# A gated mixer on one core: the first row pair by Strassen too, with scaling, softmax factors and value copies on other engines

## The chip, the cores and the metric

One core of a Trainium2 chip runs the whole program. The metric is the device time of one execution in microseconds (us); the times shown are medians of several runs. A further execution was profiled.

## The reference

Two branches share one input x of 2048 tokens by 512, and a gate mixes them, all inputs in bf16:

```python
x = A_x
g = sigmoid((x * gate_w).sum(-1, keepdims=True))
# branch A: linear attention, 32 heads of 16
q, k, v = heads(x @ wqkv)
phi_q = concat(softmax(q @ w_phi), softmax(-q @ w_phi))     # per head, 32 features
phi_k = concat(softmax(k @ w_phi), softmax(-k @ w_phi))
kv, z = phi_k^T v, sum_s phi_k
a = (phi_q kv / (phi_q z + 1e-6)) @ wo
# branch B: gated MLP with a spatial product over the tokens
z = gelu(x @ w_in)                     # 2 x 688 columns
z1, z2 = z[:, :688], layernorm(z[:, 688:])
b = (z1 * (w_sp @ z2 + b_sp)) @ w_out  # w_sp: 2048 x 2048, entries of some 0.0005
out = g * a + (1 - g) * b
```

## The kernel before, in words

Tokens are handled in 16 tiles of 128. TensorE's and ScalarE's instructions run in the order in which they are written (a manual schedule); the scheduler orders those of VectorE, GpSimd and the SyncE queue (SP) by the order of writing and by when their inputs are ready. So the place of a statement in the loops below sets what waits for what.

**Gelu stage.** For 16 tiles z2 is computed (8 matmuls, gelu by ScalarE, statistics and normalisation by VectorE into `z2all`, fp16), then for 16 tiles z1 (`z1_tile`, L278). Both write to `zp`, two PSUM banks in three buffers. During z1 `fold` (L318) multiplies w_phi into the query and key weights, on PE and with three copies by ScalarE, and `z_sum` (L397) makes eight block sums T1 to T4 of z2all on VectorE.

**Key stage, 16 steps.** Each step `tt` does `k_tile(tt + 1)` and `v_tile(tt)` on TensorE, then `kv_acc(tt - 2)`, then its share of the spatial product, and in some steps (`Q_AT`) a `q_tile`. A key tile is two exponentials by ScalarE (`ek`, both signs), one sum per head by VectorE (`zs`, L446), a reciprocal (`rk`), and two GpSimd operations that give the second half of `ek` the ratio of the two sums (`even_out`). What is then left, the factor 1/z, VectorE multiplies into the value tile `vr` (L487) as it leaves PSUM, and GpSimd writes it to vr's last columns (L485).

**Spatial product.** w_sp is loaded transposed by DMA, by pairs: pair p holds row tiles p and p + 8 in one of four ring buffers (`w_load`, tile `wsp`). The pair's four blocks A11, A12 (row tile p) and A21, A22 are multiplied by the four blocks of z2all with Strassen's scheme in Winograd's form: seven `product`s of 8 matmuls each (L563) instead of eight. They need S1 = A21 + A22, S2 = A22 - S3, S3 = A11 - A21, S4 = A12 - S2 (`w_sum`), made on VectorE in fp16. To keep fp16 in range, a pair has a level: ScalarE sums the magnitudes (`w_size`, tile `mute`, L341), a matmul with ones sums over partitions (`w_level`), and VectorE forms `wdown` and its inverse `wup`. ScalarE scales the lower half by wup (`w_scale`, L374); the upper half stays raw in bf16 and is scaled inside the two sums that use it (`w_mul_sub`, L361). Product 1, made of raw numbers, is scaled when ScalarE copies it to a second bank (`seed`). Pair 0 doesn't do this: `plain` (L527) multiplies its rows in bf16, 16 matmuls for each half row, and one VectorE instruction finishes it. The finished rows are multiplied into z1all, for Strassen's pairs by GpSimd (`gated`, L577).

`steps` lists the products by step; `work_at` lists when sizes, scalings and sums are made ready: S3 and S1 of a pair one step before its first, S2 in it, S4 one later. The products use three PSUM banks (`mm0` to `mm2`), keys, values and queries one each (`mm3` to `mm5`).

**Output stage.** The rest of the products, the attention tiles (`attn_tile`), and for each token tile the two last products and the store (`ba_tile`) alternate by the list `FILL`.

Of the kernel before, what the change touches and what calls it, by code (L numbers as in the profile page):

```python
# [14 lines left out]
P = 128  # L15
S = 2048
D = 512
# [18 lines left out]
PLAIN = (0,)  # L36
MIXED = (1, 2, 3, 4, 5, 6, 7)
# [4 lines left out]
def kernel(  # L42
# [53 lines left out]
    wsum = pers.tile([P, NP, 2], FP32, name="wsum")  # L96
    wsum16 = pers.tile([P, NP], BF16, name="wsum16")
# [57 lines left out]
    nc.sync.dma_start(out=brow[0:NT, :], in_=B_b_sp.rearrange("(t p) -> t p", p=P))  # L155
    heads = A_w_phi.rearrange("(kc u) e f -> u e kc f", u=8)
    for qk in (1, 0):
        nc.sync.dma_start_transpose(
            out=wqkT[:, qk * NDT:(qk + 1) * NDT, :], in_=A_wqkv[:, qk * D:(qk + 1) * D])
        for u in range(8 if qk == 1 else 0):  # L160
            us = slice(u * DH, (u + 1) * DH)
            nc.sync.dma_start(out=wphi[us, :, us], in_=heads[u])
    nc.sync.dma_start(out=wv_sb[:, :, :], in_=A_wqkv[:, 2 * D:3 * D].rearrange("(dt p) n -> p dt n", p=P))
# [9 lines left out]
    for p in range(3):  # L173
        w_load(p)
# [163 lines left out]

    def w_size(p, h):
        mute = ring.tile([P, NT * P], BF16, name="mute", bufs=1)  # L340
        nc.scalar.activation(  # L341
            out=mute[:, :],
            in_=wraw[p][:, h * NT:(h + 1) * NT, :].rearrange("p s c -> p (s c)"),
            func=AF.Abs, accum_out=wsum[:, p, h:h + 1])
        if h == 1:
            nc.scalar.activation(
                out=wsum16[:, p:p + 1], in_=wsum[:, p, 1:2], func=AF.Identity, bias=wsum[:, p, 0:1])

    def w_level(p, ps):
        nc.tensor.matmul(ps[:, 0:1], lhsT=ones_sq[:, :], rhs=wsum16[:, p:p + 1], start=True, stop=True)  # L350
        with tc.high_priority():
            nc.vector.tensor_scalar(
                out=wdown[:, p:p + 1], in0=ps[:, 0:1], scalar1=LEVEL, scalar2=1e-30,
                op0=ALU.mult, op1=ALU.max)
            nc.vector.reciprocal(out=wup[:, p:p + 1], in_=wdown[:, p:p + 1])  # L355

    HALVED = (5, 6)

    def w_mul_sub(out, raw, p, minus):
        for c in (slice(0, HS // 2), slice(HS // 2, HS)) if p in HALVED else (slice(0, HS),):  # L360
            nc.vector.scalar_tensor_tensor(  # L361
                out=out[:, c, :], in0=raw[:, c, :], scalar=wup[:, p:p + 1], in1=minus[:, c, :],
                op0=ALU.mult, op1=ALU.subtract)

    def w_part(p, name):
        if name in ("S2", "S3"):
            return wmix[p][:, 0 if name == "S3" else 1]
        b = {"A11": 0, "A12": 1, "S4": 1, "S1": 2, "A21": 2, "A22": 3}[name]
        w = wraw[p] if name in ("A11", "A12") else wraw[p].bitcast(FP16)
        return w[:, b * HS:(b + 1) * HS, :]  # L370

    def w_scale(p):
        tail = wraw[p][:, NT:2 * NT, :].rearrange("p s c -> p (s c)")
        nc.scalar.activation(out=tail.bitcast(FP16), in_=tail, func=AF.Copy, scale=wup[:, p:p + 1])  # L374

    def w_sum(p, k):
        if k == 3:
            wmix[p] = ring.tile([P, 2, HS, P], FP16, name="wmix", bufs=2)
        a21, a22, s2, s3 = (w_part(p, name) for name in ("A21", "A22", "S2", "S3"))
        if k == 1:  # L380
            nc.vector.tensor_tensor(out=a21, in0=a21, in1=a22, op=ALU.add)
        elif k == 2:
            nc.vector.tensor_tensor(out=s2, in0=a22, in1=s3, op=ALU.subtract)
        elif k == 3:
            w_mul_sub(s3, w_part(p, "A11"), p, a21)
        else:
            w_mul_sub(w_part(p, "S4"), w_part(p, "A12"), p, s2)
# [15 lines left out]
    with tc.manual_schedule(engines={mybir.EngineType.PE, mybir.EngineType.Activation}):  # L403
        z2_first_two()
        for tt in range(2, NT):
            z2_tile(tt)
            if tt % 4 == 3:
                z2_norm(list(range(tt - 3, tt + 1)))
        b_T()
        turn["zp"] += 1  # L410
        for tt in range(NT):
            z1_tile(tt)
            if tt % 2 == 1:
                z_sum(tt // 2 // 4, tt // 2 % 4)
            if tt in (6, 11):
                later = fold(1 if tt == 6 else 0)
            if tt in (7, 8, 12, 13):
                later.pop(0)()

# [32 lines left out]
    def k_tile(tt, bank):  # L452
        ek, z = expo(kvp, "ek", 5, tt, wk_p, bank_tile(bank))
        rk = kvp.tile([P, H, 2], FP32, name="rk", bufs=3)
        nc.vector.reciprocal(out=rk[:], in_=z[:])  # L455
        even_out(ek, z, rk[:, :, 1])
        return ek, rk

    def even_out(e, z, rz):
        ratio = work.tile([P, H], FP32, name="ratio")  # L460
        nc.gpsimd.tensor_tensor(out=ratio[:], in0=z[:, :, 0], in1=rz, op=ALU.mult)  # L461
        nc.gpsimd.tensor_tensor(  # L462
            out=e[:, :, 1, :], in0=e[:, :, 1, :],
            in1=ratio[:, :, None].to_broadcast([P, H, DH]), op=ALU.mult)

# [3 lines left out]
    def q_tile(n, ps):  # L469
        eq, z = expo(work, "eq", 3, token(n), wq_p, ps)  # L470
        rq = work.tile([P, H], FP32, name="rq")
        nc.vector.reciprocal(out=rq[:], in_=z[:, :, 1])
        even_out(eq, z, rq[:])
        eqT = work.tile([P, 8, P], BF16, name="eqT", bufs=7)
        nc.sync.dma_start_transpose(out=eqT[:, :, :], in_=eq[:].rearrange("p h a f -> p (h a f)"))  # L475
        eqTs[n] = eqT

    def v_tile(tt, rk, bank):
        v_ps = bank_tile(bank)
        for dt in range(NDT):  # L480
            nc.tensor.matmul(v_ps[:, :], lhsT=xT[:, dt, tt * P:(tt + 1) * P], rhs=wv_sb[:, dt, :],  # L481
                             start=(dt == 0), stop=(dt == NDT - 1))
        vr = kvp.tile([P, 8, AW], BF16, name="vr", bufs=4)
        r0 = rk[:, :, 0].rearrange("p (u h) -> p u h", u=8)
        nc.gpsimd.tensor_copy(out=vr[:, :, 64:AW], in_=r0)  # L485
        with tc.high_priority():
            nc.vector.tensor_tensor(  # L487
                out=vr[:, :, 0:64].rearrange("p u (h d) -> p u h d", d=DH),
                in0=v_ps[:, :].rearrange("p (u h d) -> p u h d", u=8, d=DH),
                in1=r0[:, :, :, None].to_broadcast([P, 8, NG, DH]),  # L490
                op=ALU.mult,
            )
        return vr
# [33 lines left out]
    def plain(t, j):  # L527
        x = bank_tile(next_turn("mm", 2))[:, 0:HF]
        h = t // HS
        for st in range(NT):  # L530
            nc.tensor.matmul(  # L531
                x, lhsT=wraw[t % HS][:, h * NT + st, :], rhs=z2all[:, st, j * HF:(j + 1) * HF],
                start=(st == 0), stop=(st == NT - 1))
        zu = z1_of(t, j * HF, (j + 1) * HF)
        nc.vector.scalar_tensor_tensor(
            out=zu, in0=x, scalar=bT[:, t:t + 1], in1=zu, op0=ALU.add, op1=ALU.mult)

    LOAD_AT = {3: 1, 4: 4, 5: 7, 6: 10, 7: 13}
    SIZE_AT = {1: (0, 1, 2), 2: (2, 3, 4), 6: (14, 16, 17), 7: (18, 19, 20)}
# [8 lines left out]
    def seed(p):  # L548
        xbanks[p, 1] = bank_tile(X_TAGS[1])
        nc.scalar.activation(  # L550
            out=xbanks[p, 1][:, 0:HF], in_=xbanks[p, 0][:, 0:HF], func=AF.Copy,
            scale=wup[:, p:p + 1])
# [4 lines left out]
    def product(p, k):  # L557
# [23 lines left out]
        elif k == 2:  # L581
            o = mix_tile("c", 3)
            nc.scalar.activation(out=o, in_=x, func=AF.Identity, bias=bT[:, t0:t0 + 1])
# [93 lines left out]
    for p in range(NP):  # L677
        n, after = len(steps), MIXED[MIXED.index(p) + 1:][:1] if p in MIXED else ()
        if p in PLAIN:
            steps += [[(plain, t, j)] for t in (p, p + HS) for j in range(2)]  # L680
            continue
# [4 lines left out]
        if not follow:  # L686
            first.append(middle.pop(0))
        steps += [first, middle, [(product, p, 4), (product, p, 3)]]
        for k, lag in ((3, -1), (1, -1), (2, 0), (4, 1)):
            at(n + lag, w_sum, p, k)  # L690
        s0, s1, s2 = SIZE_AT.get(p, (n - 5, n - 4, n - 3))
        at(s0, w_size, p, 0)
        at(s1, w_size, p, 1)
        at(s2, w_scale, p)
    for p in range(3, NP):
        at(LOAD_AT[p], w_load, p)

# [14 lines left out]
    Q_AT = (1, 3, 6, 9, 12, 15)  # L712
    with tc.manual_schedule(engines={mybir.EngineType.PE, mybir.EngineType.Activation}):
# [3 lines left out]
        for tt in range(NT):  # L717
# [3 lines left out]
            late = steps[0][0][0] is product and steps[0][0][2] in (1, 6)  # L721
            if not late:
                prepare(tt, w_size)
            ek, rk = ks.pop(tt)
            pend.append((tt, ek, v_tile(tt, rk, V_BANK if tt != 1 else X_TAGS[2])))
# [26 lines left out]
    with tc.manual_schedule(engines={mybir.EngineType.PE, mybir.EngineType.Activation}):  # L752
# [29 lines left out]
        for n in range(3):  # L782
            products(1 + (n > 0))
            attn_tile(n)
            q_next()
# [52 lines left out]
```

## Time and profile before

| | |
|---|---|
| median of 3 runs | 199.93 us (199.37 to 200.1) |
| the profiled execution | 199.89 us |
| its span, first to last instruction | 198.2 us |
| TensorE clock granted | 1.0 throughout |
| busy: PE, DVE, ACT, POOL | 193.4, 144.4, 136.2, 88.2 us |
| z1's gelu stage | 24.1 to 44.1 us |
| key stage | 44.1 to 125.5 us |

PE is TensorE's matmuls, PEld its weight loads, DVE VectorE, ACT ScalarE, POOL GpSimd, SP the SyncE queue that issues most DMAs. Busy time counts an instruction from its start to its end, so time in which it is held up after its start is in it too. A row of the page's second part divides the span into 40 slices of 4.95 us and gives the busy tenths of each. The chain follows the last instruction back through what released each step.

### The profile page before, as it was taken

To read this page: it belongs to the slowest core of one execution; us is meant where nothing else is said; L and a number is where in the kernel's file an instruction comes from. 1 tells how busy PE (TensorE), PEld (TensorE's weight loads), DVE (VectorE), ACT (ScalarE), POOL (GpSimd) and SP (SyncE) were. 2 spreads that over 40 slices of the span, in tenths; PEclk is the share of its full clock that TensorE was granted. 3 is DMA by queue.
4 is the path that set the end of the run, shared out by engine and by line. 5 is a ranking of instruction groups with operands and counts; after the bars stand their busy time and mean duration, and the time that the engine had idled before them with its cause. 6 is when DMAs were issued, how large, how long until landed. Compare 5 with 4: busy or idle time off the path is not lost.

```text
span 198.2 us, 3988 instructions
## 1 busy us (share of the span) xinstructions
PE 193.4 (98%) x1466; PEld 115.6 (58%) x1484; DVE 144.4 (73%) x268; ACT 136.2 (69%) x216; POOL 88.2 (45%) x132
## 2 busy tenths in 40 slices
PE   8999999999999999999999999999999999999994
PEld 4666666665555665565565566665555555654542
DVE  4478977914989999798798796998968569554300
ACT  3466667889899679789789788569675476232222
POOL 6021023000552685885795788645536245420400
PEclk9999999999999999999999999999999999999999
DMA  6799479999803930750870666697688898595261
GB/s 193 134 190 218 86 156 194 207 202 208 244 3 64 200 58 0 159 109 0 160 107 3 132 133 69 143 205 146 138 161 181 113 220 149 119 149 132 65 147 53
DMA packets 89210, 26.50 MB, mean 134 GB/s; under 512 B 84536, under 2 KB 89064, under 8 KB 89192
## 3 DMA queue, kind: packets, MB, share of 16 engines
q1 hardware_dynamic: 86448, 23.32, 62.2%
q10 hardware_dynamic: 2600, 2.42, 5.0%
q0 software_dynamic: 144, 0.52, 0.8%
q8 instruction: 11, 0.18, 0.4%
q14 instruction: 7, 0.06, 0.1%
HBM read 3.45 MB, written 2.10 MB: 28 GB/s over the span
## 4 chain that ended last, share of the span: by engine, by line
PE 92%; SPq 2%; DMA 2%; DVE 1%; issue 1%; DVEq 0%
PE mm L563 27%; PE zp L208 19%; PE mm L438 14%; PE mm L634 8%; PE mm L481 7%; PE mm L629 6%; PE mm L531 5%; DMA oT<-o 2%; PE kvacc L498 2%; PE at L604 2%; SPq L524 1%; PE zp L239 1%; DVE o L615 1%; SPq L475 1%; PE zp L327 0%
## 5 line engine op out<-in xcount | busy, mean ns | idle before, releaser
L208 PE MATMUL zp<-w_z,xT 128*128 128x344 bf16 (+1 forms) x254 | 38.5, 311 | 0.0
L577 POOL TENSOR_TENSOR z1all<-c,z1all 128x344 bf16<-128x344 f32 x28 | 25.5, 916 | 21.0 <-DVE c L570 7.2
L563 PEld LDWEIGHTS <-wsp 128*128 128x128 f16 (+1 forms) x280 | 26.6, 98 | 13.9
L208 PEld LDWEIGHTS <-xT 128*128 128x128 bf16 x254 | 24.4, 98 | 12.3 <-DMA xT<-in_A_x_dram 0.4
L563 PE MATMUL mm<-z2all,wsp 128*128 128x344 f16 x168 | 27.9, 309 | 0.0
L341 ACT ACTIVATE mute<-wsp 128x2048 bf16<-128x2048 bf16 x14 | 26.8, 1914 | 0.4 <-ACT ob L646 0.4
L446 DVE TENSOR_REDUCE zs<-eq 128x64 f32<-128x1024 bf16 x16 | 19.3, 1209 | 7.5 <-ACT eq L442 7.5
L646 ACT ACTIVATE ob<-mm,g_inv 128x512 bf16<-128x512 f32 (+1 forms) x16 | 10.9, 680 | 19.8 <-PE mm L634 17.8
L446 DVE TENSOR_REDUCE zs<-ek 128x64 f32<-128x1024 bf16 x16 | 19.2, 1203 | 7.2 <-ACT ek L442 7.2
L634 PE MATMUL mm<-w_out_sb,uT 128*128 128x512 bf16 (+2 forms) x101 | 23.3, 366 | 0.1
L461 POOL TENSOR_TENSOR ratio<-zs,rk 128x32 f32<-128x32 f32 x16 | 8.2, 511 | 32.8 <-DVE rk L455 29.7
L442 ACT ACTIVATE eq<-mm 128x512 bf16<-128x512 f32 x32 | 17.3, 593 | 6.9 <-PE mm L438 6.4
L563 PE MATMUL mm<-zmix,wmix 128*128 128x344 f16 x112 | 18.6, 309 | 0.0
L563 PE MATMUL mm<-zmix,wsp 128*128 128x344 f16 x112 | 18.6, 309 | 0.0
L462 POOL TENSOR_TENSOR eq<-eq,ratio 128x512 bf16<-128x512 bf16 x16 | 17.4, 1089 | 1.3
L438 PEld LDWEIGHTS <-xT 128*128 128x128 bf16 x128 | 11.8, 98 | 10.5
L462 POOL TENSOR_TENSOR ek<-ek,ratio 128x512 bf16<-128x512 bf16 x16 | 17.9, 1119 | 0.0
L442 ACT ACTIVATE ek<-mm 128x512 bf16<-128x512 f32 x32 | 17.3, 603 | 0.5 <-PE mm L438 0.2
L374 ACT ACTIVATE wsp<-wsp,wup 128x2048 f16<-128x2048 bf16 x7 | 14.0, 2001 | 4.5 <-DVE wup L355 4.5
L223 ACT ACTIVATE z2raw<-zp 128x688 bf16<-128x688 f32 x16 | 11.9, 745 | 7.4 <-PE zp L208 7.0
L481 PE MATMUL mm<-wv_sb,xT 128*128 128x512 bf16 x62 | 16.3, 379 | 0.1
L629 PE MATMUL mm<-wo_t,oT 128*128 128x512 bf16 (+2 forms) x65 | 16.3, 366 | 0.2
(100 smaller groups left out, 308.2 us busy)
## 6 DMA issues: line engine op xcount, KB each, us to landing
out_dram<-ob ACTq DMA_DIRECT2D x14, 128.0 KB, 2.5
w_z<-in_B_w_in_dram SPq DMA_DIRECT2D x2, 344.0 KB, 5.8
w_out_sb<-in_B_w_out_dram SPq DMA_DIRECT2D x1, 640.0 KB, 4.8
wv_sb<-in_A_wqkv_dram SPq DMA_DIRECT2D x1, 512.0 KB
wo_t<-in_A_wo_dram POOLq DMA_DIRECT2D x1, 512.0 KB, 5.8
w_z<-in_B_w_in_dram ACTq DMA_DIRECT2D x2, 172.0 KB, 3.4
w_z<-in_B_w_in_dram SPq DMA_DIRECT2D x2, 172.0 KB, 3.3
wsp<-in_B_w_sp_dram SPq DMA_TRANSPOSE x16, 5.2
```

What stands on the lines that cost most here:

```text
L208: nc.tensor.matmul(zp[:, j, 0:n], lhsT=xT[:, dt, tt * P:(tt + 1) * P], rhs=wt[:, dt, j * HF:j * HF + n], start=(dt == 0), stop=(dt == NDT ...
L341: nc.scalar.activation(out=mute[:, :], in_=wraw[p][:, h * NT:(h + 1) * NT, :].rearrange("p s c -> p (s c)"), func=AF.Abs, accum_out=wsum[: ...
L374: nc.scalar.activation(out=tail.bitcast(FP16), in_=tail, func=AF.Copy, scale=wup[:, p:p + 1])
L438: nc.tensor.matmul(ps[:, :], lhsT=xT[:, dt, tt * P:(tt + 1) * P], rhs=w[:, dt, :], start=(dt == 0), stop=(dt == NDT - 1))
L442: nc.scalar.activation(out=e[:, :, a, :], in_=ps[:, :].rearrange("p (h f) -> p h f", f=DH), func=AF.Exp, scale=1.0 - 2.0 * a)
L446: nc.vector.tensor_reduce(out=z[:].rearrange("p h a -> p (h a)"), in_=e[:].rearrange("p h a f -> p (h a) f"), axis=AX.X, op=ALU.add,)
L462: nc.gpsimd.tensor_tensor(out=e[:, :, 1, :], in0=e[:, :, 1, :], in1=ratio[:, :, None].to_broadcast([P, H, DH]), op=ALU.mult)
L481: nc.tensor.matmul(v_ps[:, :], lhsT=xT[:, dt, tt * P:(tt + 1) * P], rhs=wv_sb[:, dt, :], start=(dt == 0), stop=(dt == NDT - 1))
L563: nc.tensor.matmul(x, lhsT=w_part(p, wa)[:, st, :], rhs=zsums[zb][:, st, :], start=(k in OPENS and st == 0), stop=(st == HS - 1), skip_gro ...
L577: nc.gpsimd.tensor_tensor(out=zu, in0=o, in1=zu, op=ALU.mult)
L629: nc.tensor.matmul(acc, lhsT=oTs[n][:, g, :], rhs=wo_t[:, g, c0:c1], start=start and g == 0, stop=stop and g == NG - 1)
L634: nc.tensor.matmul(acc, lhsT=uTs[n][:, ft, :], rhs=w_out_sb[:, ft, c0:c1], start=start and ft == 0, stop=stop and ft == NFT - 1)
```

## The change

- Pair 0 goes by Strassen's seven products like the others; `plain` is gone. Its steps are the same four: products 1 and 5; 2; 6, 1 of pair 1, and 7; 4 and 3.
- `w_scale` runs on VectorE, in two halves of 2048 columns, over the whole pair; all four block sums are then plain sums of fp16, and `seed` is a plain copy.
- The key tile gets both factors by one GpSimd multiplication over its 1024 columns (rk of both signs); `ratio` and the write to vr are gone for keys. The value tile is only copied, by ScalarE, into one of four fixed buffers whose last columns are set to one at the start.
- The size of pair 0's second half and of both halves of pair 1 is a maximum by VectorE (`w_peak`); the rest stay on ScalarE. `w_level` adds the two halves with two matmuls.
- Pair 0's size, level, scaling, S3 and S1, and pair 1's peaks, lie in z1's gelu stage, whose VectorE order is now manual as well. z_sum and the second fold come earlier.
- The load of pair 0 goes ahead of the value weights, and all four first pairs are loaded at the start. Seven query tiles instead of six lie in the key stage, at other steps.

```diff
-PLAIN = (0,)
-MIXED = (1, 2, 3, 4, 5, 6, 7)
+MIXED = tuple(range(NP))
...
+    load_wqk(0)
+    w_load(0)
+    nc.sync.dma_start(
+        out=wv_sb[:, :, :], in_=A_wqkv[:, 2 * D:3 * D].rearrange("(dt p) n -> p dt n", p=P))
+    for p in range(1, 4):
         w_load(p)
...
+    def w_peak(p, h):
+        nc.vector.tensor_reduce(
+            out=wsum[:, p, h:h + 1], in_=w_half(p, h), axis=AX.X, op=ALU.max,
+            apply_absolute_value=True)
...
     def w_level(p, ps):
-        nc.tensor.matmul(ps[:, 0:1], lhsT=ones_sq[:, :], rhs=wsum16[:, p:p + 1], start=True, stop=True)
+        for h in range(2):
+            nc.tensor.matmul(
+                ps[:, 0:1], lhsT=ones_sq[:, :], rhs=wsum[:, p, h:h + 1], start=h == 0, stop=h == 1)
...
     def w_scale(p):
-        tail = wraw[p][:, NT:2 * NT, :].rearrange("p s c -> p (s c)")
-        nc.scalar.activation(out=tail.bitcast(FP16), in_=tail, func=AF.Copy, scale=wup[:, p:p + 1])
+        for h in range(2):
+            w = w_half(p, h)
+            nc.vector.tensor_scalar(
+                out=w.bitcast(FP16), in0=w, scalar1=wup[:, p:p + 1], scalar2=None, op0=ALU.mult)
+
+    W_SUMS = {3: ("S3", "A11", ALU.subtract, "A21"), 1: ("S1", "A21", ALU.add, "A22"),
+              2: ("S2", "A22", ALU.subtract, "S3"), 4: ("S4", "A12", ALU.subtract, "S2")}
...
+        out, a, op, b = W_SUMS[k]
+        nc.vector.tensor_tensor(out=w_part(p, out), in0=w_part(p, a), in1=w_part(p, b), op=op)
...
+    with tc.manual_schedule(engines={
+            mybir.EngineType.PE, mybir.EngineType.Activation, mybir.EngineType.DVE}):
         for tt in range(NT):
             z1_tile(tt)
-            if tt % 2 == 1:
-                z_sum(tt // 2 // 4, tt // 2 % 4)
-            if tt in (6, 11):
+            if tt in (1, 2, 3, 4, 6, 7, 8, 9):
+                n = tt - 1 - (tt > 5)
+                z_sum(n // 4, n % 4)
+            if tt in (6, 10):
                 later = fold(1 if tt == 6 else 0)
-            if tt in (7, 8, 12, 13):
+            if tt in (7, 8, 11, 12):
                 later.pop(0)()
+            if tt == 5:
+                w_peak(0, 1)
+            if tt == 9:
+                w_size(0, 0)
+            if tt == 12:
+                w_level(0, zp_tile()[:, 0, :])
+                w_scale(0)
+                w_sum(0, 3)
+                w_sum(0, 1)
+                w_peak(1, 0)
+                w_peak(1, 1)
...
-        even_out(ek, z, rk[:, :, 1])
-        return ek, rk
+        ekf = ek[:].rearrange("p h a f -> p (h a) f")
+        nc.gpsimd.tensor_tensor(
+            out=ekf, in0=ekf,
+            in1=rk[:].rearrange("p h a -> p (h a)")[:, :, None].to_broadcast([P, 2 * H, DH]),
+            op=ALU.mult)
+        return ek
...
-        nc.gpsimd.tensor_copy(out=vr[:, :, 64:AW], in_=r0)
-        with tc.high_priority():
-            nc.vector.tensor_tensor(
...
+        vr = vrs[tt % len(vrs)]
+        nc.scalar.copy(
+            out=vr[:, :, 0:64], in_=v_ps[:, :].rearrange("p (u c) -> p u c", u=8))
...
-    LOAD_AT = {3: 1, 4: 4, 5: 7, 6: 10, 7: 13}
-    SIZE_AT = {1: (0, 1, 2), 2: (2, 3, 4), 6: (14, 16, 17), 7: (18, 19, 20)}
+    LOAD_AT = {4: 3, 5: 6, 6: 9, 7: 12}
+    SIZE_AT = {1: (None, None, 1), 6: (13, 14, 16), 7: (17, 18, 19)}
...
-    Q_AT = (1, 3, 6, 9, 12, 15)
+    Q_AT = (3, 5, 7, 9, 11, 13, 15)
...
-            q_next()
+            if n in (0, 2):
+                q_next()
```

## The prediction

> **What bounds the kernel now.** The page first: engine shares, then the row of slices.
>
> ```profile
> PE 193.4 (98%) x1466; PEld 115.6 (58%) x1484; DVE 144.4 (73%) x268; ACT 136.2 (69%) x216; POOL 88.2 (45%) x132
> ...
> PE   8999999999999999999999999999999999999994
> PEld 4666666665555665565565566665555555654542
> DVE  4478977914989999798798796998968569554300
> ```
>
> TensorE never lacks work from the second slice to the last but one. So only removed matmuls can save time, and any wait put in front of TensorE costs its full length. VectorE stands idle once, in slice 9, and is then near full for most of the next 14. The windows show how close this is to a second bound (columns: window, then busy us and instruction count of PE, PEld, DVE, ACT, POOL, then clock, DMA share, GB/s).
>
> ```profile
> 44.10:65.50 21.40, 21.24 (x142) 12.18 (x143) 17.02 (x27) 20.21 (x30) 7.80 (x16) 1.00 0.60 136
> 65.50:85.00 19.50, 19.40 (x137) 11.81 (x138) 17.71 (x28) 15.25 (x22) 13.83 (x20) 1.00 0.52 106
> 85.00:105.00 20.00, 19.89 (x147) 12.14 (x148) 18.04 (x26) 17.12 (x27) 14.95 (x19) 1.00 0.47 82
> ```
>
> TensorE lacks 0.1 us in each, at full clock, while VectorE works 91% and 90% of the later two and GpSimd 71% and 75%. The busy time of these two holds waits for each other. The timelines of both around 70 us show it (start, duration, engine, line).
>
> ```profile
> 69.72 0.21 POOL L485 CAST vr<-rk 128x32 bf16<-128x32 f32 x1
> 69.89 2.12 POOL L462 TENSOR_TENSOR ek<-ek,ratio 128x512 bf16<-128x512 bf16 x1
> 71.97 1.82 POOL L577 TENSOR_TENSOR z1all<-c,z1all 128x344 bf16<-128x344 f32 x1
> ```
> ```profile
> 69.81 1.28 DVE L361 SCALAR_TENSOR_TENSOR wmix<-wsp,wup 128x1024 f16<-128x1024 bf16 x1 [0.37 <-ACT wsp L374]
> 71.01 2.08 DVE L361 SCALAR_TENSOR_TENSOR wsp<-wsp,wup,wmix 128x1024 f16<-128x1024 bf16 x1
> ```
>
> L462 takes 1.05 us elsewhere; here it begins 0.08 us after VectorE's block sum, takes 2.12, and ends 1.0 us after that sum. The second sum, queued meanwhile, takes 2.08 instead of 1.2; L577, behind it, takes 1.82 instead of 0.84. They run strictly in turn, each waiting out the other. VectorE's L728, which adds a constant to 16 columns, likewise took 0.44 us and ended with the GpSimd operation that it met, though it reads one SBUF tensor only. Reductions (L446, 1.15 to 1.22 us in every meeting) don't wait. So what the change moves onto VectorE and GpSimd is priced with this turn-taking.
>
> **The matmuls.** The chain has each plain group of 16 matmuls at 2.33 us, each product of 8 at 1.17. Pair 0 goes from four plain groups (9.33) to seven products (8.17): -1.17. The level becomes two one-column matmuls for eight pairs instead of one for seven, 9 more; steps with a level have a 0.28 us key accumulation in the chain, others 0.26, so 0.02 to 0.03 each: +0.2. (Their own row, 0.167 us each if nothing overlapped, gives +1.5 as upper end.) Queries move between steps, 16 in all as before: nothing. Net -1.0, of 199.89 us for the profiled execution (span 198.2, 1.7 around it; the median is 199.93). That is all the change can win.
>
> **The gelu stage (24 to 44 us).** ScalarE has 0.64 us of gelu per tile against TensorE's 1.17, so 0.53 spare; a fold's copies take 0.91 + 2 x 0.53. The new size pass at tile 9 takes 1.89 (mute from start to next start, 48.28 to 50.17), just ahead of the fold. gelu 10 then starts at 39.1 instead of 37.7; TensorE has three zp buffers, and tile 12 waits for gelu 10 (0.3), tile 13 for gelu 11 behind the fold copy (0.3): +0.6, between 0 and 1.9. VectorE's part hides in its idle 40 to 47.5 us: peak of a half by the 1.13 us per 1024 columns of L446, 2.2 us; level; scale; two sums; two more peaks of pair 1. That is done by 48.6 to 50.2, where the two key sums ran at 47.47 before: nothing for TensorE yet, but VectorE enters the next stage 1 to 3 us late. The loads keep their cover: pair 0 landed at 35.2 and 37.5, two us earlier without wv in front; wv comes some 6 us before its first use at 46. load 4 on SP waits for pair 0's last product with query transposes behind it, which are wanted only after 124 us.
>
> **Costs per pair, from then on (three steps, 15.2 us of TensorE).** Taken from VectorE: 3 value multiplications of 0.60 (and 0.49 twice for each plain row, once), and two multiply-subtracts at 1.2 become plain sums at 0.62 (L381). Added: two scalings of 2048 columns. Nearest row is L292, same types, 688 columns, 0.454 us: no less than that, and no more than 0.15 + 0.30 x 2048/688 = 1.05; since four in a row start every 0.37 us, less than the 0.53 ns a column of L400 plus its fixed part would allow, I take 0.75, toward the lower end. VectorE's own work: 3 keys at 1.61, 1.3 queries at 1.4, two plus at 0.49, level 0.15, four sums 2.5, two scalings 1.5: 11.8.
>
> [...]
>
> GpSimd drops ratio 0.25, cast 0.21, half tile 1.05 and gets one operation of 1024 columns: slope (1.05-0.25)/480 gives 1.9, two half tiles 2.1; I take 1.9. Per pair 3 x 1.9 + 4 x 0.84 + 1.3 x 1.3 = 10.8, or 71% of 15.2. The sum hardly moves, but the grain does: what VectorE meets is 1.9 long, not 0.25 to 1.05.
>
> [...]
>
> Turn-taking: VectorE now has six operations of the waiting kind per pair (two scalings, four sums) instead of four. A GpSimd operation is under way 71% of the time with on average 0.70 left (sum of squares over twice the sum): 6 x 0.71 x 0.70 = 3.0. The second scaling follows the first with a key multiplication let in between, whole and not average: +1.2. So 11.8 + 4.2 = 16.0 against 15.2: VectorE falls behind by 0.8 per pair, +2.4 over pairs 2 to 4.
>
> **Steps 1 to 3** are the tightest, since pair 0's sums have no plain stretch to hide behind. From VectorE free at 48.6: two key sums, two reciprocals, a third sum, S2 of pair 0 to 54.0, reciprocal to 54.4, then the scaling of pair 1, waiting out a key multiplication to 55.9, done 56.5; TensorE wants it at 55.9: +0.7. Then S4 of pair 0 waits out the next key multiplication (1.9), and the addition that frees bank mm2 for pair 0's last product stands behind S4 and pair 1's S3 and S1, its own input being late behind the 1.89 size pass on ScalarE: +1.9, one GpSimd operation (0 if the addition goes first, 3.4 if all three sums stand before it). ScalarE itself loses 14 us of scaling and gets 16 value copies of 0.53: lighter. After 124 us VectorE and GpSimd thin out: nothing.
>
> Sum: -1.0 + 0.6 + 0.7 + 1.9 + 2.4 = +4.6, so 204.5.
>
> **The rivals.** *The cover holds.* VectorE's order lets the sums fall in GpSimd's pauses as it does now (in the trace the two sums often begin 0.15 us before GpSimd's ratio and win the turn). Point of decision: waits under 3.4 us per pair and the addition ahead of S4. For it: VectorE's bare work falls by about 1 us per pair, and the four present sums lose little. Against it: the grain of 1.9. It gives 199.89 - 1.0 = 198.9, at most 0.6 more; faster than before. 0.26, of which a quarter beats the bound below.
>
> *VectorE becomes the bound outright.* Scaling at 1.05, key multiplication at 2.1, each of the six waiting out 1.2 on average: 12.4 + 7.2 = 19.6 against 15.2, +4.4 for each of three pairs, less what a stopped TensorE lets GpSimd finish (half): +6.6 in place of 2.4, so 208.7. 0.24.
>
> *The opening alone stalls.* Pairs 2 to 4 keep pace: 4.6 - 2.4 = +2.2, 202.1. 0.15.
>
> *The saving is not there*, because pair 0's level comes too late: size or peak landing 3 us later would hold TensorE between tiles 12 and 13, +3, 202.9. The landings speak against it: 0.03.
>
> **How the numbers follow.** My forecast has 0.32; with the others, slower has 0.74. Half a per cent, 1.0 us, is about what a measurement of this kernel can tell from no change; the most that can be won is just that, so faster gets 0.06 and same 0.20. The forecast's own range is 202.5 (no wait of the addition) to 207 (3.4 for it, scaling at 1.05). The whole range runs from 199.0, with the cover holding and half of its chance inside, to 210, the outright bound with 1.3 us for the level's upper end.
>
> **What would show it.** In the changed kernel's page PE's busy time should be about 192.5 and its share under 97%; the waits should name PE behind DVE (wsp of the scaling, c of the plus) with 1 to 3 us each between 55 and 125 us; the scalings and f16 sums should have a mean far over their shortest, GpSimd's 1024-column ek row about 1.9 at best; DVE's windows over 95%. The gelu stage should show two waits of 0.3 us for ScalarE. I am wrong if PE keeps 98%, if the sums' means stay within 0.2 us of their shortest, or if PE waits for ScalarE or a load instead.

## The result, and the profile after

The changed kernel takes 213.15 us (median of 6 runs, 211.6 to 213.47) against 200.0 for the kernel before in the same comparison: a ratio of 1.0631, interval 1.0572 to 1.069. It is slower, by 13 us and not by the 4.6 that were forecast. The profiled execution took 213.01 us, span 211.3.

The page of the changed kernel, its busy times and the slices of PE, DVE and the granted clock:

```profile
PE 196.7 (93%) x1485; PEld 115.7 (55%) x1485; DVE 161.9 (77%) x271; ACT 131.0 (62%) x221; POOL 97.0 (46%) x108
...
PE   7999999999776999998999997994999999999994
...
DVE  3377987999999799899799797896789757632500
...
PEclk9999999999999999999999999998799999999999
```

PE has fallen from 98% to 93%, with holes in slices 11 to 13, 19, 25 and 28, and in slices 28 and 29 the clock itself was reduced. VectorE, idle once in slice 9 before, is near full from slice 8 to 13. The windows of the changed kernel from the key stage on (columns as before: window, then PE, PEld, DVE, ACT, POOL, clock, DMA share, GB/s):

```profile
45.00:65.00 20.00, 17.23 (x115) 9.68 (x113) 19.93 (x24) 14.21 (x24) 9.09 (x5) 1.00 0.51 112
65.00:85.00 20.00, 18.07 (x128) 10.59 (x126) 18.68 (x24) 15.10 (x26) 13.67 (x11) 1.00 0.39 66
85.00:105.00 20.00, 19.00 (x141) 11.28 (x140) 17.96 (x25) 15.16 (x27) 15.93 (x14) 1.00 0.51 109
105.00:125.00 20.00, 20.00 (x147) 11.90 (x145) 18.76 (x25) 17.31 (x29) 17.68 (x14) 1.00 0.49 93
125.00:145.00 20.00, 16.87 (x145) 10.53 (x143) 16.04 (x27) 13.26 (x21) 12.88 (x15) 1.00 0.63 129
```

In the first window VectorE works 19.93 of 20 us and TensorE lacks 2.8. Then VectorE has slack again, yet TensorE still lacks 1.9, 1.0 and, after 125 us, 3.1. Which instructions wait, PE's timeline says (start, duration, what; in brackets the idle time before it and what ended it):

```profile
40.38 1.33 PE L211 MATMUL zp<-w_z,xT 128*128 128x344 bf16 x8 [0.33 <-ACT z1all L283]
41.92 3.66 PE L211 MATMUL zp<-w_z,xT 128*128 128x344 bf16 x24 [0.19 <-ACT z1all L283]
56.66 0.43 PE L510 MATMUL kvacc<-vr,ek 128*128 128x68 bf16 x8 [1.48 <-POOL ek L469]
59.55 1.34 PE L562 MATMUL mm<-z2all,wsp 128*128 128x344 f16 x8 [1.29 <-DVE wsp L375]
67.14 1.33 PE L562 MATMUL mm<-z2all,wsp 128*128 128x344 f16 x8 [1.94 <-DVE c L569]
99.21 1.33 PE L562 MATMUL mm<-z2all,wsp 128*128 128x344 f16 x8 [1.00 <-DVE c L569]
130.73 1.33 PE L562 MATMUL mm<-z2all,wsp 128*128 128x344 f16 x8 [1.31 <-DVE c L569]
146.22 0.42 PE L603 MATMUL at<-kvz,eqT 128*128 128x68 bf16 x8 [3.00 <-DVE o L614]
```

Eight waits make 10.5 us: 0.5 in the gelu stage, 7.0 in the key stage, 3.0 in the output stage. Straight behind the last one, from 146.65 to 150.06 us, the granted clock was 0.50; these 3.41 us are worth 1.7:

```profile
145.00:147.00 2.00, 0.78 (x10) 0.54 (x11) 1.68 (x3) 1.33 (x2) 0.04 (x1) 0.91 0.68 155
147.00:150.10 3.10, 3.10 (x8) 1.06 (x7) 3.10 (x5) 0.00 (x0) 1.31 (x2) 0.51 0.34 77
150.10:155.00 4.90, 4.90 (x36) 2.69 (x35) 2.75 (x5) 1.81 (x4) 0.84 (x1) 1.00 0.68 146
```

With the 1.0 won by the matmuls the account is -1.0 + 0.5 + 7.0 + 3.0 + 1.7 = 11.2. The z1 stage began 0.6 later (first matmul at 24.50 us against 23.91). This start lay between 23.67 and 24.50 in all the kernels run here, and at 23.67 and 23.71 in two with the same code up to there (`half_scaling`, `three_ut`), so it belongs to the execution rather than to the change. That makes 11.8 of 13.1.

The other 1.3 comes with the eight waits. A wait is counted from the modelled end of the matmul before it, but in a full stream the next matmul begins ahead of that end: a product at 138.24 us lasts 1.33, and the next one begins at 139.40, 0.17 before its end. So each wait costs some 0.16 us more than its idle time, 1.3 for the eight, which closes the account.

**The key stage.** The groups of the changed kernel (busy us, mean ns), first the key multiplication on GpSimd, then the scaling and three of the four sums on VectorE:

```profile
L469 POOL TENSOR_TENSOR ek<-ek,rk 128x1024 bf16<-128x1024 bf16 x16 | 34.3, 2145 | 22.3 <-DVE rk L467 20.7 <-PE mm L450 1.7
...
L375 DVE TENSOR_SCALAR wsp<-wsp,wup 128x2048 f16<-128x2048 bf16 x16 | 16.9, 1092 | 0.1
L385 DVE TENSOR_TENSOR wsp<-wsp,wmix 128x1024 f16<-128x1024 f16 x8 | 12.7, 1587 | 0.0
L385 DVE TENSOR_TENSOR wmix<-wsp 128x1024 f16<-128x1024 f16 x8 | 9.0, 1131 | 0.0
L385 DVE TENSOR_TENSOR wmix<-wsp,wmix 128x1024 f16<-128x1024 f16 x8 | 7.8, 973 | 0.0
```

The three sums are S4, S3 and S2. The shortest scaling of this execution took 0.65 us and the shortest sum 0.62; their means are 1.09 and, for S4, 1.59. Taken over all 16 scalings and 32 sums, what lies above the shortest is 7 + 15 = 22 us. Most of it, not all, is VectorE waiting for GpSimd: 21 of them lie in scalings and sums that overlap a GpSimd instruction, while the 13 sums that meet none took 0.62 to 0.69 (the first two, at 45 and 46 us, 0.69). The timelines of VectorE and GpSimd at the opening show one such meeting, and why tile 0 came late:

```profile
46.75 4.47 DVE L352 TENSOR_REDUCE wsum<-wsp 128x1 bf16<-128x2048 bf16 x2
51.14 0.68 DVE L385 TENSOR_TENSOR wmix<-wsp,wmix 128x1024 f16<-128x1024 f16 x1
51.74 2.34 DVE L458 TENSOR_REDUCE zs<-ek 128x64 f32<-128x1024 bf16 x2
...
57.54 3.19 DVE L375 TENSOR_SCALAR wsp<-wsp,wup 128x2048 f16<-128x2048 bf16 x2
...
64.19 2.41 DVE L385 TENSOR_TENSOR wmix<-wsp,wmix 128x1024 f16<-128x1024 f16 x1
66.52 0.57 DVE L569 SCALAR_TENSOR_TENSOR c<-mm,wdown,u 128x344 f32<-128x344 f32 x1
```
```profile
54.68 4.26 POOL L469 TENSOR_TENSOR ek<-ek,rk 128x1024 bf16<-128x1024 bf16 x2 [15.52 <-DVE rk L467]
...
60.14 2.38 POOL L469 TENSOR_TENSOR ek<-ek,rk 128x1024 bf16<-128x1024 bf16 x1
63.75 2.29 POOL L469 TENSOR_TENSOR ek<-ek,rk 128x1024 bf16<-128x1024 bf16 x1 [1.23 <-DVE rk L467]
```

S2 of pair 1 begins at 64.19, behind a key multiplication begun at 63.75 that ends at 66.04, and itself ends 0.56 after that: 2.41 us for 0.62 of work, so 1.79 of waiting. The addition c stands next in VectorE's queue, and product 3 of pair 0 (PE, 67.14) waits for it.

**The output stage.** SyncE's queue of the changed kernel:

```profile
131.13 2.19 SPq L495 DMA_TRANSPOSE eqT<-eq  x1
133.42 8.01 SPq L536 DMA_TRANSPOSE uT<-z1all  x6
141.53 1.25 SPq L495 DMA_TRANSPOSE eqT<-eq  x1
142.89 1.20 SPq L623 DMA_TRANSPOSE oT<-o  x1
```

The transposes uT bring branch B's rows into the form for the output products; six are queued in a row, and the first is used at 148.0. In the kernel before five of them ran from 120.6 to 128.5 us, begun before the first attention tile (125.3). Now they start at 133.4, only 1.1 us before the first attention tile (134.5), and stand in front of the transpose oT of an attention result that was ready near 137. VectorE's third o (L614) waits for that transfer to free its buffer, holding VectorE's queue, and TensorE's fourth attention tile waits for the o.

### The profile page after: what moved, and what is told of

It is laid out like the page before. It is cut to its first block, busy times and chain, and to the rows that moved or that the text cites. A ratio compares the mean times of both kernels' runs of the same rounds, so it can differ in the third digit from the quotient of the medians.

```text
span 211.3 us, 3983 instructions
## 1 busy us (share of the span) xinstructions
PE 196.7 (93%) x1485; PEld 115.7 (55%) x1485; DVE 161.9 (77%) x271; ACT 131.0 (62%) x221; POOL 97.0 (46%) x108
## 4 chain that ended last, share of the span: by engine, by line
PE 49%; DVE 35%; ACT 6%; issue 3%; DMA 3%; POOL 3%; SPq 0%; DVEq 0%
PE mm L562 18%; PE mm L633 10%; PE mm L450 7%; PE mm L628 7%; DVE bn L229 6%; DVE zs L458 5%; DVE wsp L375 4%; DVE wsp L385 4%; DVE wmix L385 4%; DVE z2all L295 3%; DVE zmix L398 3%; DVE wsum L352 2%; PE at L603 2%; ACT ek L454 2%; POOL rstd L293 2%
## 5 line engine op out<-in xcount | busy, mean ns | idle before, releaser
L469 POOL TENSOR_TENSOR ek<-ek,rk 128x1024 bf16<-128x1024 bf16 x16 | 34.3, 2145 | 22.3 <-DVE rk L467 20.7
L562 PEld LDWEIGHTS <-wsp 128*128 128x128 f16 x320 | 30.2, 98 | 21.8 <-issue 5.1
L576 POOL TENSOR_TENSOR z1all<-c,z1all 128x344 bf16<-128x344 f32 x32 | 29.6, 933 | 19.4 <-DVE c L569 13.3
L562 PE MATMUL mm<-z2all,wsp 128*128 128x344 f16 x192 | 31.9, 309 | 5.5 <-DVE c L569 4.2
L562 PE MATMUL mm<-zmix,wmix 128*128 128x344 f16 x128 | 21.3, 309 | 0.0
L562 PE MATMUL mm<-zmix,wsp 128*128 128x344 f16 x128 | 21.3, 309 | 0.0
L477 POOL TENSOR_TENSOR ratio<-zs,rq 128x32 f32<-128x32 f32 x16 | 4.8, 302 | 31.4 <-DVE rq L492 18.7
L546 ACT ACTIVATE c<-mm,bT,wdown 128x344 f32<-128x344 f32 x16 | 10.3, 646 | 10.8 <-PE mm L562 10.5
L375 DVE TENSOR_SCALAR wsp<-wsp,wup 128x2048 f16<-128x2048 bf16 x16 | 16.9, 1092 | 0.1
L633 PEld LDWEIGHTS <-uT 128*128 128x128 bf16 x102 | 10.1, 101 | 12.2 <-issue 1.7
```

The source lines that it names most:

```text
L375: nc.vector.tensor_scalar(out=w.bitcast(FP16), in0=w, scalar1=wup[:, p:p + 1], scalar2=None, op0=ALU.mult)
L469: nc.gpsimd.tensor_tensor(out=ekf, in0=ekf, in1=rk[:].rearrange("p h a -> p (h a)")[:, :, None].to_broadcast([P, 2 * H, DH]), op=ALU.mult)
L562: nc.tensor.matmul(x, lhsT=w_part(p, wa)[:, st, :], rhs=zsums[zb][:, st, :], start=(k in OPENS and st == 0), stop=(st == HS - 1), skip_gro ...
L576: nc.gpsimd.tensor_tensor(out=zu, in0=o, in1=zu, op=ALU.mult)
L633: nc.tensor.matmul(acc, lhsT=uTs[n][:, ft, :], rhs=w_out_sb[:, ft, c0:c1], start=start and ft == 0, stop=stop and ft == NFT - 1)
```

## The experiments

The theory after the result: a GpSimd multiplication of 1.9 us makes VectorE's scalings and sums wait their turn, and additions behind them come late; the late end of the key stage then sets off the output stage's wait and the half clock. The rivals: VectorE's new work and its order alone do it, whatever GpSimd runs; or pair 0's opening does it; or the output stage's loss is a matter of its own. All edits are to the changed kernel unless it says otherwise.

**The key multiplication left out** (`no_key_factor`; the keys then lack their softmax factor):

```diff
-        nc.gpsimd.tensor_tensor(out=ekf, in0=ekf, in1=..., op=ALU.mult)
```

> The changed kernel without GpSimd's multiplication of ek by rk (the key factors are left out of the result); the order of VectorE's instructions stays the same, one by one. Theory A (turn-taking: VectorE's six waiting operations per pair stand behind 2 us operations of GpSimd): the 7.0 us that TensorE lacks between 45 and 134 us go, the means of the scaling and of the block sums fall to within 0.15 us of their shortest (0.72 and 0.62), and what follows late in the output stage (3.0 of waiting, 1.7 of half clock) goes too: 201 to 203 us. Theory B (VectorE simply has too much to do, the scaling above all): its work and order are unchanged, so 211 to 213. Theory C (ScalarE's value copies come late): also 211 to 213.

Measured 203.12 us, ratio to the kernel before 1.0149 (1.0128 to 1.0169). One GpSimd instruction for each key tile carries 10 of the 13 us, TensorE's direct wait of 1.5 for ek included. VectorE's instructions and their order are the same, so its order alone is not the cause. The groups of this kernel:

```profile
L375 DVE TENSOR_SCALAR wsp<-wsp,wup 128x2048 f16<-128x2048 bf16 x16 | 14.2, 921 | 0.1
L385 DVE TENSOR_TENSOR wsp<-wsp,wmix 128x1024 f16<-128x1024 f16 x8 | 7.5, 940 | 0.0
L385 DVE TENSOR_TENSOR wmix<-wsp 128x1024 f16<-128x1024 f16 x8 | 6.7, 835 | 0.0
```

S4 fell from 1.59 to 0.94 us without an edit to it. Time above the shortest fell from 22 to 10 us over the kernel. Against the expectation, the means did not all come down to within 0.15 us of the shortest: the scaling stayed 0.27 above it and S4 0.32. Left are the gelu stage's 0.5 and waits of 0.9 before product 1 of pair 1, and 0.35 and 1.6 before attention tiles.

**The same multiplication in four pieces of 256 columns** (`key_in_four`), 0.75 us each in the mean:

```diff
-        nc.gpsimd.tensor_tensor(out=ekf, ...)
+        for c in range(4):
+            cs = slice(16 * c, 16 * c + 16)
+            nc.gpsimd.tensor_tensor(out=ekf[:, cs, :], in0=ekf[:, cs, :], ...)
```

> The changed kernel with GpSimd's key multiplication in four pieces of 256 columns, VectorE's order unchanged. GpSimd's own work rises by 3 x 0.25 us per key tile, 12 us in all. Theory A with the length of one operation as its cause: a meeting costs at most 0.65 us instead of 2.0, TensorE's missing time in the key stage falls from 7.0 to 2 or 3, total 206 to 209. If the amount of GpSimd's work is the cause: 213 or more. Theory B: 213.

Measured 208.18, ratio 1.0418 (1.0379 to 1.0457). GpSimd now works longer (107.5 us against 97.0), and still the kernel gains 5 us: S4's mean is 1.08, the waits before products 1 and 3 are gone but for 0.3. So for these waits it is the length of what VectorE meets, not GpSimd's load. The wait for ek of tile 0 remains in four fragments (1.65 in all), behind which the matmuls of the profiled execution ran at half pace (the product begun at 57.20 us took 2.48, others 1.33), and 3.2 before the attention tile; the mean clock was 0.983.

**The keys' factors and the value tiles as they were before** (`old_key_factors`), all else changed:

```diff
-        nc.gpsimd.tensor_tensor(out=ekf, ...)
-        return ek
+        even_out(ek, z, rk[:, :, 1])
+        return ek, rk
...
-        nc.scalar.copy(out=vr[:, :, 0:64], ...)
+        nc.gpsimd.tensor_copy(out=vr[:, :, 64:AW], in_=r0)
+        nc.vector.tensor_tensor(out=vr[:, :, 0:64]..., in0=v_ps..., in1=r0..., op=ALU.mult)
```

> The changed kernel with the keys' factors as before: ratio and half tile on GpSimd, VectorE multiplies the value tile (16 x 0.68 us more work), GpSimd writes its last columns. Theory A: VectorE's waits of 20 us in scaling and sums fall by more than the 10.7 us that it gets, total 207 to 211. Theory B (VectorE's own work): 10 us more on the engine that sets the pace, 217 or more.

Measured 208.66, ratio 1.0419 (1.039 to 1.0447). The size is the one expected, but in the key stage it comes from a single wait. PE's and VectorE's timelines, and a window of it:

```profile
55.35 1.87 PE L493 MATMUL mm<-wv_sb,xT 128*128 128x512 bf16 x4 [4.16 <-DVE vr L499]
```
```profile
46.56 4.47 DVE L352 TENSOR_REDUCE wsum<-wsp 128x1 bf16<-128x2048 bf16 x2
...
54.67 0.63 DVE L499 TENSOR_TENSOR vr<-mm,rk 128x512 bf16<-128x512 f32 x1
```
```profile
54.20:61.10 6.90, 5.75 (x19) 2.46 (x19) 4.96 (x10) 0.64 (x1) 5.09 (x10) 0.51 0.01 2
```

Pair 1's two peaks, 4.5 us on VectorE, keep the first value tile in its only bank until 55.3; TensorE stands for 4.2 us. In this window the clock was 0.51 in the mean, and TensorE worked 5.75 of the 6.90 us, worth 2.9. No other wait of the key stage is left, and 1.3 before attention tiles. So two parts of the change hang together, by this timeline: with these peaks on VectorE, the value tile of tile 0 isn't emptied there in time.

**Three uT buffers for six** (`three_ut`), which alters only what stands in SyncE's queue:

```diff
-    NUT = 6
+    NUT = 3
```

> The changed kernel with three uT buffers instead of six; orders of TensorE, VectorE, ScalarE and GpSimd stay the same, only SyncE's queue changes. Theory: the 3.0 us wait of the fourth attention tile (for o, which waits for the first oT transpose, issued 6 us late behind six uT transposes) and the 3.4 us at half clock behind it go: 3.0 + 1.7 less, 208 to 209 us, clock 1.0 throughout. Rival: VectorE's lateness holds o anyway, 212 to 213.

Measured 208.1, ratio 1.0402 (1.0387 to 1.0418). SyncE's queue and PE's waits of this kernel:

```profile
132.26 3.90 SPq L536 DMA_TRANSPOSE uT<-z1all  x3
137.16 1.23 SPq L495 DMA_TRANSPOSE eqT<-eq  x1
138.49 1.21 SPq L623 DMA_TRANSPOSE oT<-o  x1
```
```profile
PE mm L562 <- DVE c L569: 4.2, 3, 1.9
...
PE at L603 <- DVE o L614: 0.9, 1, 0.9
```

The fourth attention tile waits 0.9 instead of 3.0 and the clock stays full (1.0 in the mean), while the key stage's waits (4.2 for c) are what they were. So 2.1 us of waiting and 1.7 of clock, out of the 5 us between the two kernels, lay in the order of one DMA queue; the opening's wait was 0.4 shorter here, and z1 began 0.8 earlier.

The key stage's lateness alone doesn't explain that order. With the key multiplication left out, the last key accumulation was done at 126.1 us, near the 124.3 of the kernel before, and six uT still stood ahead of the first oT, with 1.6 us of waiting. In the changed kernel the uT stand behind the transpose eqT of the sixth query tile (131.13), whose matmuls ran at 120.6 and which GpSimd finished at 131.1; in the kernel before the sixth query tile came two steps later and its eqT (128.54) went behind five uT. The new places of the query tiles are thus a candidate that no run moves by itself.

**Pair 0 as before** (`pair0_plain`), with the rest of the change:

```diff
-MIXED = tuple(range(NP))
+PLAIN = (0,)
+MIXED = tuple(range(1, NP))
...
-                w_level(0, zp_tile()[:, 0, :])
-                w_scale(0)
-                w_sum(0, 3)
-                w_sum(0, 1)
                 w_peak(1, 0)
```

> The changed kernel with pair 0 as before: sixteen plain matmuls for each half row, no size, level, scaling or sums for it; all else of the change stays (pair 1's peaks in the gelu stage too). Theory A: the waits of the opening (1.5, 1.3 and 1.9 us between 55 and 68 us) and the gelu stage's 0.5 go, those of pairs 2 to 4 (1.0 and 1.3) and of the output stage (3.0, with 1.7 of half clock) stay, the matmuls' 1.0 us come back: 208 to 210. Theory D (pair 0 by Strassen is itself the cause, the rest harmless): 200 to 202.

Measured 206.93, ratio 1.0337 (1.0277 to 1.0397), below the 208 to 210 expected. The opening's waits are gone, and the 1.0 before pair 2's product 3 too; 1.3 before a product 3 at 124 and 3.0 before the attention tile, with matmuls at half pace behind it (four of 512 columns in 1.90 us for 1.03), are left. Pair 0 by Strassen costs 6 us net of the 1.0 that it wins, but is not the whole.

**The parts alone, put into the kernel before.** First the key factors on GpSimd with value copies on ScalarE (`only_keys`):

```diff
-        even_out(ek, z, rk[:, :, 1])
-        return ek, rk
+        nc.gpsimd.tensor_tensor(out=ekf, in0=ekf, in1=..., op=ALU.mult)
+        return ek
...
+        nc.scalar.copy(out=vr[:, :, 0:64], ...)
```

> The kernel before with one part of the change: both key factors in one GpSimd multiplication of 1024 columns, value tiles copied by ScalarE. VectorE loses 16 x 0.68 us; its four waiting operations per pair are longer (two of 1.2) and meet 2 us operations. Theory A: waits of about 1 us in half of the meetings, 10 us in all, against 11 us of work less: VectorE as full as before, 200 to 203 us. If a long GpSimd operation is enough by itself: 207 or more.

Measured 205.36, ratio 1.0257 (1.0213 to 1.0302), between what the two theories gave. The turn-taking needs no new scaling: the two sums with a multiplication in them wait as well (means of 2.07 and 1.51 us for 1024 columns, 1.41 and 1.38 before). Waits of 0.6, 0.75 and 0.6 reach TensorE in the key stage, and 2.5 at the attention tile, again behind a run of uT in SyncE's queue. Then the scaling on VectorE with plain sums, keys as before (`only_scaling`; in this kernel pairs 6 and 7 have product 1 read w_sp before it is scaled):

```diff
-        nc.scalar.activation(out=tail.bitcast(FP16), in_=tail, func=AF.Copy, scale=wup[:, p:p + 1])
+        for h in range(2):
+            nc.vector.tensor_scalar(out=w.bitcast(FP16), in0=w, scalar1=wup[:, p:p + 1], ...)
...
-            w_mul_sub(s3, w_part(p, "A11"), p, a21)
+            nc.vector.tensor_tensor(out=s3, in0=w_part(p, "A11"), in1=a21, op=ALU.subtract)
```

> The kernel before with one part of the change: scaling of the whole pair on VectorE, all block sums plain. VectorE's work per pair stays (2.4 less in the sums, 1.5 more in scaling), ScalarE loses 14 us; six waiting operations meet GpSimd operations of at most 1.05 us. Theory A: waits stay near those of before, 199.5 to 201. Theory B (the scaling on VectorE is what costs): 205 or more.

Measured 201.38, ratio 1.0062 (1.0038 to 1.0087). Alone, it costs 1.3 us and wins nothing: its sums have means of 0.67 to 0.80.

**Half of the scaling back on ScalarE** (`half_scaling`), for pairs 2 to 7:

```diff
+            if h == 1 and p > 1:
+                nc.scalar.activation(out=w.bitcast(FP16), in_=w, func=AF.Copy, scale=wup[:, p:p + 1])
+                continue
```

> The changed kernel with the lower half of the scaling on ScalarE from pair 2 on (2.0 us each there), so five waiting operations per pair instead of six. Theory A: each of VectorE's second scalings with its wait took 1.1 us; the waits of pairs 2 to 4 (1.0 and 1.3) shrink or go, the opening's 4.7 stay: 209 to 212. Theory C (ScalarE's lateness): 2 us more per pair on ScalarE, 215 or more.

Measured 211.0, ratio 1.054 (1.0504 to 1.0576). The two later waits for c gave way to 0.4 and 0.6 for ScalarE; the opening (1.5, 1.3, 1.9) and the attention tile (2.6) stayed; the mean clock, 0.992, is that of the changed kernel too. Relieving VectorE of one scaling for each pair takes out over half of these two waits and little of the rest.

**Pair 0 by Strassen without the losses.** `mended` keeps pair 0's products and the scaling on VectorE, but takes the old key factors, three uT buffers, the second value tile into the queries' bank, pair 1's sizes on ScalarE in steps 0 and 1, and pair 1's product 1 a step later:

```diff
-                w_peak(1, 0)
-                w_peak(1, 1)
...
-    SIZE_AT = {1: (None, None, 1), 6: (13, 14, 16), 7: (17, 18, 19)}
+    SIZE_AT = {1: (0, 1, 2), 6: (13, 14, 16), 7: (17, 18, 19)}
...
-    follow = [(product, q, 1) for q in after if q == p + 1]
+    follow = [(product, q, 1) for q in after if q == p + 1 and p > 0]
...
+            pend.append((tt, ek, v_tile(tt, rk, V_BANK if tt != 1 else Q_BANK)))
```

> A version meant to beat both: the changed kernel with the keys' factors as before, three uT buffers, the second value tile in the queries' bank, pair 1's sizes on ScalarE in steps 0 and 1 (not VectorE's peaks), and pair 1's first product in its own step 4. Theory A: the opening's wait for the value tile (4.2 us, with 3.4 lost to half clock, in the version with old factors) goes, GpSimd's operations are short: 199.5 to 201 us, with 0.5 of waits in the gelu stage against 1.0 saved in matmuls. Theory B (VectorE's own work): 205 or more.

Measured 202.18, ratio 1.0106 (1.0075 to 1.0138): 11 us faster than the change, and still 2 slower than the kernel before. Its waits are 0.5 in the gelu stage, 0.35 and 0.9 before attention tiles, and one before product 7 of pair 0, by its PE and ScalarE timelines:

```profile
54.74 1.33 PE L560 MATMUL mm<-zmix,wmix 128*128 128x344 f16 x8
56.79 1.33 PE L560 MATMUL mm<-zmix,wmix 128*128 128x344 f16 x8 [0.73 <-ACT u L544]
```
```profile
55.74 0.27 ACT L728 ACTIVATE g_el<-glog 128x16 f32<-128x16 f32 x1
56.10 0.64 ACT L544 ACTIVATE u<-mm,bT,wdown 128x344 f32<-128x344 f32 x1
```

Products 6 and 7 add up in the same bank. Product 6 ends at 56.07, ScalarE is free at 56.01 and reads the bank (u) from 56.10 to 56.74, and product 7 begins at 56.79. ScalarE isn't late: 0.73 is this reading itself, with nothing between the two products, since the version moved pair 1's product 1, which stood there, a step later. `mended2` moves the second fold to tile 12, S2 of pair 0 into the gelu stage, and gives o four buffers:

```diff
-            if tt in (6, 10):
+            if tt in (6, 12):
...
+                w_sum(0, 2)
...
+        o = work.tile([P, D], BF16, name="o", bufs=4)
```

> The mended version with the second fold two tiles later (against the gelu stage's 0.5 us), pair 0's S2 right behind its S1 (against 0.7 us at its product) and four o buffers (against the 1.3 us that the third and fourth attention tile waited): 202.2 less up to 2.5, so 199.7 to 200.7. If VectorE's order, not the buffer, holds the attention tiles: 201.

Measured 201.9, ratio 1.0105 (1.0086 to 1.0124). The gelu stage's 0.5 became 0.4. Neither the 0.73 nor the attention tiles' 0.35 and 0.9 moved, so neither S2's place nor o's buffers made them. `mended3` further gives ScalarE the lower half of the scaling of pairs 5 to 7 (`half_scaling`'s edit with `p > 4`):

> mended2 with the lower half of the scaling of pairs 5, 6 and 7 on ScalarE, which has room in the output stage: VectorE's 0.8 us with its wait leave the way of the attention tiles. 199.3 to 200.3; against the kernel before between 0.7 faster and 0.3 slower.

Measured 202.76, ratio 1.0157 (1.0122 to 1.0193), a miss: 0.6 for ScalarE at 133 us came new and the attention wait is 1.2. No version beat the kernel before. What these waits come to, 2.5 us in `mended` and 0.16 more for each of the five, exceeds the 1.0 that pair 0's matmuls can give.

## Why the prediction was right and wrong

- *The mechanism*, VectorE and GpSimd in turn with a grain of 1.9 us, held: S4's mean fell from 1.59 us to 0.94 in `no_key_factor` and to 1.08 in `key_in_four`. The key multiplication took 1.92 at best against 1.9 taken; the scaling's shortest, 0.65, lies below the 0.75 taken.
- *Gelu stage*: 0.6 forecast, 0.5 measured, at the two tiles named.
- *Step 3, the addition behind S4*: 1.9 forecast, 1.94 measured. The price of one meeting was right, but the sum that met the key multiplication was S2 of pair 1, not S4 of pair 0, and the addition's input u, forecast late, was ready at 62.7; that the figure came out so close is in part luck.
- *Pairs 2 to 4*: 2.4 forecast, 2.3 measured, for a reason that was half wrong, so the agreement is luck. Turn-taking was 3.0 to 3.8 us per pair against 4.2, and VectorE was not the bound there (it worked 18 to 19 of 20 us). The waits were not a lag of 0.8 for each pair; they fell at single points, 1.0 and 1.3, where an addition stood in the queue behind sums and reductions.
- *Step 2, the scaling of pair 1*: 0.7 forecast, 1.3 measured. TensorE waits for the first of the two scalings. That one did wait out a key multiplication, as forecast, and took 1.95 us, but it began at 57.54, 3.1 later than forecast, since VectorE entered the stage later than the 48.6 that these steps start from.
- *"TensorE: nothing yet" at the end of the gelu stage* failed. VectorE was done with the peaks at 51.2, past the forecast's 48.6 to 50.2, and steps 1 to 3 were worked out from its early end: the price of 2.2 each was right, but the first peak began only at 46.75. S2 of pair 0 came next, ahead of the key sums and not behind them. So the key multiplication of tile 0 began at 54.68 and ended after the key accumulation was due at 55.2: 1.5 us that had no term.
- *"After 124 us nothing"* failed most, by 4.7 us: 3.0 of waiting behind uT, and 1.7 of half clock. The forecast looked at the load of VectorE and GpSimd there, and not at SyncE's queue, in which the six uT came ahead of a transfer that was now due behind them. It priced moved query transposes as harmless, "wanted only after 124 us", and asked nothing of who stands before whom at that time. `three_ut` shows this step: with three uT ahead, 2.1 of the wait and the half clock are gone. What put the six there is open, as said above.
- *No term* stood for the 0.16 us that each wait costs beyond its idle time (1.3 in all). With it, the 1.5 for ek, 0.6 in step 2, 4.7 after 124 us and z1's 0.6, the distance from 4.6 to 13.1 is accounted for.
- *The signs.* PE's share fell to 93% and its waits bear the names forecast, but its busy time is 196.7 and not 192.5: 1.7 of it is half clock and 1.3 the ends of matmuls before a wait, and the profile before lacks some matmul records (324 of 512 columns in the key, value, query and output products, where the changed one has 342). VectorE was over 95% busy only in the first window (93, 90 and 94% in the next).
- One sum is off: the upper end of the forecast's own range, 207, comes to 207.8 by its terms (1.5 for the addition, 0.6 for each of three pairs).
- The rivals missed as well. *VectorE the bound outright* gave 208.7, nearest in size, but not by its mechanism: its 19.6 us per pair was never seen.

## What to carry to other kernels

When an elementwise operation is moved to an engine that takes turns with a near-full one, its length counts before its load: one operation of 1.9 us for each of 16 tiles cost 10 us of 200, and cut in four, with more work in all, 5. When a stage is forecast to end some microseconds late, read the DMA queues that follow and ask which prefetches would now stand in front of a transfer that is due: here six uT (8.01 us) stood before an oT that was ready near 137 us and began at 142.89. Then look at the clock granted around the stops: here it was 0.50 for 3.41 us behind one of 3.00, and matmuls ran at half pace behind four that add up to 1.65 us, none over 0.8.

## What the runs showed of the hardware

The forecast had no half clock within the busy kernel. In the changed kernel the granted clock was 1.00 to 146.65 us, 0.50 from there to 150.06, 3.41 us in all, and 1.00 behind it. In `old_key_factors` it was 0.51 in the mean of a window of 6.90 us, from 54.20 to 61.10.

By the waits that TensorE had there, the cases stand as follows. Half clock, or matmuls at half pace, stood at or behind waits of 3.00 us (changed kernel), 3.01 (`pair0_plain`) and 4.16 (`old_key_factors`); `half_scaling`, whose longest wait was 2.62, had a mean clock of 0.992. Behind waits of 2.46 (`only_keys`, attention tile) and 1.94 (changed kernel, before product 3 of pair 0) the matmuls ran at full pace. But in `key_in_four` they ran at half pace behind four stops of 0.18, 0.34, 0.34 and 0.79 us, 1.65 in 2.36 us. So the longest single stop doesn't sort the cases; what does was not shown.

The price can be read between executions of one kernel: three of `half_scaling` at a mean clock of 0.992 took 210.97 to 211.34 us, one at 0.999 took 209.22.
